# Moving the routing steps of a recurrence-and-experts kernel to fixed places, and moving scatters, gathers and weights ahead of a branch

## The chip, the cores and the metric

The kernel runs on one core of one Trainium2 chip. Five engines work beside each other on that core: TensorE (PE in the profile, with its weight loads listed as PEld), VectorE (DVE), ScalarE (ACT), GpSimd (POOL) and SyncE (SP), which issues most of the DMAs. Each engine runs its own instructions in order and waits on the others by semaphores. The metric is the time of one execution on the device in microseconds (us); less is better. The profile also lists the clock that TensorE was granted, as a share of its full 2.4 GHz: 1.00 is 2.4 GHz and 0.50 is 1.2 GHz.

## The reference

Three stages follow one another. The sizes are B=4 batches, H=8 heads, S=768 steps, head size D=48, so 3072 tokens of 384 numbers; E=8 experts with a hidden size of 1024; a last layer with a hidden size of 2048. All is float32.

```python
for t in range(S):                                   # per batch and head: a decayed sum of outer products
    cur = einsum('bhd,bhe->bhde', u * k[t], v[t])
    y[t] = einsum('bhd,bhde->bhe', r[t], state + cur)
    state = w[t][..., None] * state + einsum('bhd,bhe->bhde', k[t], v[t])
x = y rearranged to 3072 x 384
e = argmax(x @ w_gate); gate = softmax(x @ w_gate)[e]; eom = sigmoid(x @ w_output_gate)
for each expert: out[e == expert] = gate * eom[expert] * (relu(x[e == expert] @ w1[expert]) @ w2[expert])
return relu(out @ w_in) ** 2 @ w_out
```

## The kernel before

**Attention in units.** A unit is one batch and one pair of heads: 16 units, four to a batch. The loop `for t in range(-3, LU + 1)` (L803) is a software pipeline: turn `t` does parts of units `t-1`, `t`, `t+1`, `t+2` and `t+3`, each by a call `at(unit, "part")`. In a unit DVE scans the decays (`suf` L686, then a reciprocal and `ff` L694), makes `kT` (L705) and `rA` (L711) from transposes that PE left in the PSUM tile `pt`, scans the states into `St` (L754), sums the bonus `g` (L720) and writes the rows of the output `xr` (L776, "rows_out"). PE makes transposes (L675), the scores `pa` (L741, in two halves), and the results `py` from the scores (L764) and from the states (L770). POOL makes the causal cut of the scores (the two affine selects on `A`, L744), the products `g` (L715, L716) and `gv` (L724). In every turn but the one that follows a batch's first pair of heads, PE transposes parts of `xr` ("turn_x", L675 too) for the routing. The order of instructions on each engine is that of the code.

**Routing in steps.** When a batch is done, `route_steps` (L161) works out for its 768 tokens which expert each goes to, and its place there. It is a generator. Every `yield` ends a step, and the loop of units calls `route_step()` at a few places per turn. The steps are: the product with both gates (`wcat`, L169) into `lt`; its transposes into `lg`; the maximum `mx` and `z`; then `cand`, `m`, `oh` and the scan `inc` (L190 to L197) on DVE; PE's two matmuls `pk` on `inc` and `oh` (L202, L203), which ACT copies to `kv`, and DVE's `zo`, `zs`, `sg` (L208 to L213); the places `ex`, `bof`, `rk`, `dst`, `dsi` (L217 to L225); the factor `tail` (L227 to L229), which ACT copies into `xr` (L231); and the running counts `cum` and `vals`. With that the rows of the batch go to the table `x_rows` in DRAM by six indirect DMAs on POOL (`scatter_step`, L265).

**First block of experts.** After the loop `blkA` gathers 320 rows of expert 0 (three indirect DMAs on POOL, L409) that belong to the first three batches, scales them, turns them (L440) and runs them through the expert: `up(f)` (nine matmuls into `ph`, then ACT's `hh` and DVE's `hl`) and `down(f)` (nine matmuls into `po`) for f = 0 to 7. Under `up` and `down` the fourth batch is routed. The table `under` says which step follows which of them; `conv(f)` there makes the weights of f (ACT writes `w1h`, `w2h`, DVE `w1l`, `w2l`; called a weight pair below). `finish_steps` (called by `fin`) then makes the table of blocks: `key` to `bvals` (L299 to L307), `bei` to `flag` (L310 to L321) and the list of rows `gi` (L280 to L288). `flag` is read by all engines for a branch on a rare case (L916, L917; not taken with these inputs). Behind the branch come the rest of `blkA`, the second block `blk0` and blocks 1 to 7, whose expert numbers are read from `bei`.

## Time and profile before

| | |
|---|---|
| time, three runs | 904.79, 908.29 (median), 912.22 us |
| profiled execution | 910.06 us, span 908.4 us |
| granted TensorE clock, mean | 0.951 |
| busy: PE, DVE, ACT, POOL | 94%, 62%, 42%, 40% of the span |
| attention, routing of three batches | to about 214 us |
| first block and routing of the fourth batch | about 214 to 257 us |
| blocks of experts, then the last layer | about 257 to 500 us, 500 to 908 us |

The profiled execution is a single one, 1.8 us above the median. A share such as PE's 94% is an average over stages; it includes time in which matmuls run at half the clock. The table of windows and the timelines tell more: where an idle time of an engine stands in brackets in a row, it is the time just before that row, with the instruction that ended it.

### The profile page before, as it was taken

How to read it: one execution, taken by the hardware profiler on the slowest of the kernel's cores; microseconds unless marked ns; L12 is line 12 of the kernel's file. 1: busy time of each engine (PE TensorE's matmuls, PEld its weight loads, DVE VectorE, ACT ScalarE, POOL GpSimd, SP SyncE). 2: the span in 40 equal slices, each digit the busy share in tenths (PEclk: the TensorE clock that was granted, in tenths of full speed). 3: DMA queues.
4: the chain of work that ended last, by engine and by line, in shares of the span. 5: the costliest groups of instructions: out<-in, count | busy, mean ns of one | idle time of the engine just before them, and what ended most of it. 6: DMA issues, size and time to landing. Idle time of an engine off the chain costs nothing.

```text
span 908.4 us, 14382 instructions
## 1 busy us (share of the span) xinstructions
PE 850.1 (94%) x5276; PEld 770.1 (85%) x5276; DVE 561.1 (62%) x1087; ACT 377.4 (42%) x793; POOL 363.3 (40%) x398
## 2 busy tenths in 40 slices
PE   5998989996869999989999999999999999999995
PEld 4888879885758898989998889999898899999985
DVE  5779786874636766876882577777874344343342
ACT  4553545514325455454553443434333333333321
POOL 5773755733234435552554532322322122222111
PEclk9997997967979999999999999999999999999998
DMA  9855586101049667866555432223221230231110
GB/s 191 159 106 106 127 218 148 42 27 49 35 148 210 162 142 242 241 182 188 179 183 105 140 112 86 90 70 97 78 70 39 93 105 20 85 105 34 38 44 35
DMA packets 157331, 102.86 MB, mean 113 GB/s; under 512 B 112316, under 2 KB 140908, under 8 KB 157252
## 3 DMA queue, kind: packets, MB, share of 16 engines
q1 hardware_dynamic: 151396, 86.99, 36.6%
q0 software_dynamic: 4912, 14.65, 4.6%
q8 instruction: 43, 0.70, 0.3%
q10 hardware_dynamic: 944, 0.22, 0.1%
q14 instruction: 36, 0.29, 0.1%
HBM read 79.34 MB, written 22.50 MB: 112 GB/s over the span
## 4 chain that ended last, share of the span: by engine, by line
PE 58%; issue 6%; DVE 3%; POOL 2%; DMA 2%; ACT 1%; POOLq 0%; SPq 0%; DVEq 0%; ACTq 0%
PE ph L359 9%; PE ph L360 9%; PE ph L361 9%; PE po L359 8%; PE po L361 8%; PE po L360 8%; PE px L361 2%; PE px L359 2%; PE px L360 2%; PE px L440 1%; DMA wo_f<-caf 1%; DMA x2r<-x_cols 1%; POOL out_dram L1142 1%; DVE gg L1120 0%; ACT gh L353 0%
## 5 line engine op out<-in xcount | busy, mean ns | idle before, releaser
L1120 DVE SCALAR_TENSOR_TENSOR gg<-ph,rl 128x512 f32<-128x512 f32 x96 | 66.2, 690 | 114.3 <-ACT rl L1118 114.0
L1118 ACT ACTIVATE rl<-ph 128x512 f32<-128x512 f32 x96 | 57.4, 598 | 159.2 <-PE ph L361 156.7
L354 DVE TENSOR_TENSOR gl<-gg,gh 128x512 fp32r<-128x512 f32 x96 | 66.7, 695 | 65.9 <-ACT gh L353 43.3
L353 ACT CAST gh<-gg 128x512 fp32r<-128x512 f32 x96 | 59.6, 621 | 88.9 <-DVE gg L1120 88.9
L354 POOL TENSOR_TENSOR w1l<-w1r,w1h 128x384 fp32r<-128x384 f32 x56 | 59.8, 1075 | 77.6 <-ACT w1h L353 77.5
L350 ACT ACTIVATE hh<-ph 128x320 fp32r<-128x320 f32 (+7 forms) x64 | 32.4, 506 | 117.7 <-PE ph L361 116.4
L359 PE MATMUL po<-hh,w2h 128*128 128x320 f32 (+7 forms) x192 | 69.5, 362 | 6.9 <-DVE yT L483 5.2
L354 DVE TENSOR_TENSOR w2l<-w2r,w2h 128x384 fp32r<-128x384 f32 x64 | 62.5, 978 | 20.8 <-ACT w2h L353 19.1
L351 DVE SCALAR_TENSOR_TENSOR hl<-ph,hh 128x320 fp32r<-128x320 f32 (+7 forms) x64 | 36.8, 575 | 51.2 <-ACT hh L350 51.1
L360 PE MATMUL po<-hl,w2h 128*128 128x320 f32 (+7 forms) x192 | 67.4, 351 | 0.7 <-DVE hl L351 0.5
L361 PE MATMUL po<-hh,w2l 128*128 128x320 f32 (+7 forms) x192 | 67.2, 350 | 0.0
L1066 POOL TENSOR_TENSOR caf<-caf,cbf 128x384 f32<-128x384 f32 x32 | 32.4, 1014 | 52.7 <-DVE cbf L1065 52.6
L764 PE MATMUL py<-vN,A 128*128 128x48 f32 x384 | 52.1, 299 | 0.0
L764 PEld LDWEIGHTS py<-vN,A 128*128 128x128 f32 x384 | 51.4, 218 | 0.1
L1142 POOL DMA_INDIRECT out_dram<-ob,tokc x24 | 23.7, 987 | 67.7 <-DVE ob L1141 63.8
L359 PEld LDWEIGHTS po<-hh,w2h 128*128 128x128 f32 x192 | 36.5, 190 | 10.1 <-DVE yT L483 6.6
L744 POOL TENSOR_SCALAR_AFFINE_SELECT A<-A 128x768 f32<-128x768 f32 x32 | 27.8, 869 | 42.2 <-ACT A L743 38.4
L741 PE MATMUL pa<-rA,kT 64*128 64x128 f32 x384 | 37.4, 326 | 1.3 <-ACT A L743 1.3
L743 ACT COPY A<-pa 128x384 f32<-128x384 f32 x64 | 27.6, 483 | 26.6 <-PE pa L741 26.2
L360 PEld LDWEIGHTS po<-hl,w2h 128*128 128x128 f32 x192 | 36.5, 190 | 2.4 <-DVE hl L351 1.4
L705 DVE TENSOR_TENSOR kT<-pt,suf 128x384 f32<-128x384 f32 x32 | 16.3, 549 | 34.7 <-PE pt L675 34.7
L265 POOL DMA_INDIRECT x_rows<-xr,dsi x24 | 24.5, 1022 | 32.6 <-ACT xr L231 28.9
(802 smaller groups left out, 2556.0 us busy)
## 6 DMA issues: line engine op xcount, KB each, us to landing
w1r<-in_moe_w_dram SPq DMA_DIRECT2D x16, 768.0 KB, 6.6
w2r<-in_moe_w_dram SPq DMA_DIRECT2D x16, 768.0 KB, 8.5
x2r<-x_cols SPq DMA_DIRECT2D x12, 768.0 KB, 5.2
cq<-in_moe_w_in_dram SPq DMA_DIRECT2D x16, 384.0 KB, 5.8
cq<-in_moe_w_out_dram SPq DMA_DIRECT2D x16, 384.0 KB, 5.1
wD<-in_w_dram SPq DMA_DIRECT2D x32, 144.0 KB, 3.5
kN<-in_k_dram SPq DMA_DIRECT2D x32, 144.0 KB, 3.6
rN<-in_r_dram SPq DMA_DIRECT2D x32, 144.0 KB, 3.1
```

The lines of the kernel that those rows point to most:

```text
L350: nc.scalar.activation(hi, src, AF.Relu)
L351: nc.vector.scalar_tensor_tensor(lo, src, 0.0, hi.bitcast(F32), op0=ALU.max, op1=ALU.subtract)
L353: nc.scalar.copy(hi, src)
L354: lo_eng.tensor_tensor(lo, src, hi.bitcast(F32), op=ALU.subtract)
L359: nc.tensor.matmul(out_, a_of(ah), b_of(bh), start=start, stop=False)
L360: nc.tensor.matmul(out_, a_of(ah), b_of(bl), start=False, stop=False)
L361: nc.tensor.matmul(out_, a_of(al), b_of(bh), start=False, stop=stop)
L741: nc.tensor.matmul(pa[j][:, ci], self.kT[pp, hf * HC + ci], self.rA[pp, hf * HC + ci], start=True, stop=True)
L764: nc.tensor.matmul(self.py[j][:, c], self.A[:, c, j], self.vN[:, c, j, :D], start=c == 0, stop=False)
L1118: nc.scalar.activation(rl, ph, AF.Relu)
L1120: nc.vector.scalar_tensor_tensor(gg, ph, 0.0, rl, op0=ALU.max, op1=ALU.mult)
L1142: ins = nc.gpsimd.indirect_dma_start(out=out[:, :], out_offset=IndirectOffsetOnAxis(ap=tokc[:, n:n + 1], axis=0), in_=ob, in_offset=None)
```

## The change

The change touches the places of existing work; no arithmetic of the case at hand is added. Each `yield` of the routing now carries a name ("turn", "scan", "rows", "mid", "end"), and `route_step(name)` in the loop of units runs a step only if the routing waits at that name. The steps `mx`, `z` and `cand` to `inc` become one step. The six scatters of the third batch stand in a row at the end of turn 14. All of `xr`'s transposes of the last unit stand ahead of those of `blkA`. Of the first block seven instead of six `up` stand ahead of the branch, and each of the weight pairs up to f = 7; so do the gather of `blk0` and the load of half of block 1's weights. The instruction that held the loads of the experts until the gather (`bel`, L1178) is gone.

```diff
@@ -50,7 +50,7 @@
     KF2 = F2 // 128
     CAPS = (128, 480, 440, 416, 404, 396, 388, 384)
     NA = 320
-    FA = 6
+    FA = 7
     NTL = 4
     XC = 480
     NXB = 8
...
@@ -169,21 +168,20 @@
                 nc.tensor.matmul(pl[32 * g:32 * g + 32, :GW], wcat[:, c], xT[:, c, g * GW:(g + 1) * GW], start=c == 0, stop=c == KD - 1)
         lt = wk.tile([96, GW], F32, name="lt")
         nc.scalar.copy(lt, pl[:96, :GW])
-        yield
+        yield 'turn'
         lg = wk.tile([128, 2 * E, NTB], F32, name="lg")
         pl = ps_t.tile([128, 512], F32, name=pn)
         for i in range(GW // 128):
             nc.tensor.transpose(pl[:, 96 * i:96 * i + 96], lt[:, 128 * i:128 * i + 128], ident[:96, :96])
         nc.scalar.copy(lg.rearrange("p m (g i) -> p i g m", g=NG),
                        pl[:, :192].rearrange("p (i g m) -> p i g m", i=2, g=NG)[:, :, :, :2 * E])
-        yield
+        yield 'scan'
         gl, ol = lg[:, :E], lg[:, E:]
         bce = lambda t: t.rearrange("p (o t) -> p o t", o=1).to_broadcast([128, E, NTB])
         mx = wk.tile([128, NTB], F32, name="mx")
         nc.vector.tensor_reduce(mx, gl.rearrange("p e t -> p t e"), axis=AX.X, op=ALU.max)
         z = wk.tile([128, E, NTB], F32, name="z")
         nc.vector.tensor_tensor(z, gl, bce(mx), op=ALU.subtract)
-        yield
         ez = wk.tile([128, E, NTB], F32, name="ez")
         nc.scalar.activation(ez, z, AF.Exp)
         cand = wk.tile([128, E, NTB], F32, name="cand")
...
@@ -196,7 +194,7 @@
         inc = wk.tile([128, E, NTB + 1], F32, name="inc")
         nc.vector.tensor_tensor_scan(out=inc.rearrange("p e t -> p (e t)"), data0=rst.rearrange("p e t -> p (e t)"),
                                      data1=ohx.rearrange("p e t -> p (e t)"), initial=0.0, op0=ALU.mult, op1=ALU.add)
-        yield
+        yield 'rows'
         pk = ps_t.tile([128, 512], F32, name=pn)
         pkv = pk[:, :E * (NTB + 1)].rearrange("p (e t) -> p e t", t=NTB + 1)
         nc.tensor.matmul(pkv, ones, inc, start=True, stop=False)
...
@@ -211,7 +209,7 @@
         sg = wk.tile([128, 2, NTB], F32, name="sg")
         nc.vector.tensor_reduce(sg[:, 0], ez.rearrange("p e t -> p t e"), axis=AX.X, op=ALU.add)
         nc.vector.tensor_scalar(sg[:, 0], sg[:, 0], 1e-9, None, op0=ALU.add)
-        yield
+        yield 'scan'
         nc.scalar.activation(sg[:, 1], zs, AF.Exp, scale=-1.0)
         ex = wk.tile([128, E], F32, name="ex")
         nc.vector.tensor_tensor_scan(out=ex, data0=ones[:, :E], data1=kv[:, :, NTB], initial=float(1 + b * S), op0=ALU.mult, op1=ALU.add)
...
@@ -223,15 +221,15 @@
         nc.vector.tensor_reduce(dst, rk.rearrange("p e t -> p t e"), axis=AX.X, op=ALU.add)
         dsi = wk.tile([128, NTB], I32, name="dsi", bufs=2)
         nc.vector.tensor_copy(dsi, dst)
-        yield
+        yield 'rows'
         nc.vector.tensor_scalar(sg[:, 1], sg[:, 1], 1.0, None, op0=ALU.add)
         nc.vector.reciprocal(sg, sg)
         nc.vector.tensor_tensor(tail[:, b, :, 0], sg[:, 0], sg[:, 1], op=ALU.mult)
-        yield LIGHT
+        yield 'mid'
         nc.scalar.copy(xr[:, :, DM:], tail[:, b])
         for c in range(NTB):
             scatters.append((xr, dsi, c, ordered))
-        yield
+        yield 'turn'
         eng = nc.gpsimd if b < B - 2 else nc.vector
         eng.tensor_tensor(cum[:, b + 1], cum[:, b], kv[:, :, NTB], op=ALU.add)
...
@@ -461,12 +459,13 @@
             self.prep_w1(f, eng, hi=hi1)
             self.prep_w2(f, eng2 or eng, hi=hi2)
-        def up(self, f):
+        def up(self, f, into=None):
             half, fo = divmod(f, KF // 2)
             ph = ps_h.tile([128, 512], F32, name="ph")
             for c in range(KD):
                 three(ph[:, :self.cap], self.w1t[half], self.x[c], lambda t: t[:, c, fo * 128:(fo + 1) * 128], lambda t: t, c == 0, c == KD - 1)
-            self.h[f] = split([self.P.hb.tile([128, 512], F32R, name="h" + q)[:, :self.cap] for q in "hl"], ph[:, :self.cap], nc.vector, relu=True)
+            self.h[f] = split(into or [self.P.hb.tile([128, 512], F32R, name="h" + q)[:, :self.cap] for q in "hl"],
+                              ph[:, :self.cap], nc.vector, relu=True)
         def down(self, f, again=False):
             half, fo = divmod(f, KF // 2)
...
@@ -581,10 +582,10 @@
     routing = []
-    def route_step(light=False):
-        if routing and (routing[0][1] or not light):
-            routing[0][1] = next(routing[0][0], 0)
-            if routing[0][1] == 0:
+    def route_step(place=None):
+        if routing and place in (None, routing[0][1]):
+            routing[0][1] = next(routing[0][0], None)
+            if routing[0][1] is None:
                 routing.pop(0)
     with ExitStack() as actx:
...
@@ -820,43 +821,41 @@
                 if t == LU:
                     blkA.prep_w(1, nc.vector)
                 scatter_step(t >= LU - 2)
-                if t == LU - 1:
-                    scatter_step(True)
-                route_step()
+                route_step("turn")
                 at(t, "bonus_v")
                 at(t - 1, "results")
                 at(t, "turn_back_k")
                 at(t + 1, "scan_back")
-                route_step()
+                route_step("scan")
                 at(t, "scores", 0)
                 if t == LU:
                     blkA.scale()
                 at(t - 1, "results_of_states")
                 at(t + 1, "scan_on")
+                route_step("rows")
                 at(t - 1, "rows_out")
                 scatter_step(t >= LU - 2)
                 at(t + 3, "clamp")
                 at(t, "scores", 1)
-                route_step()
-                if t == LU:
-                    blkA.prep_x(0)
-                    blkA.prep_x(1)
+                route_step("mid")
                 at(t + 2, "turn_w")
                 at(t - 1, "turn_x")
+                if t == LU:
+                    for c in range(KD):
+                        blkA.prep_x(c)
                 at(t, "states")
-                if t < LU:
-                    route_step(True)
+                route_step("end")
                 scatter_step(t >= LU - 2)
-                if t == LU - 1:
+                if t == LU - 2:
                     while scatters:
                         scatter_step(True)
+                if t == LU - 1:
                     blkA.gather()
                     blkA.prep_w(0, nc.vector)
                     nc.vector.tensor_reduce(vs, viol, axis=AX.X, op=ALU.add)
                 if t == LU:
                     pf = ps_t.tile([128, 512], F32, name="pt")
                     nc.tensor.matmul(pf[:1, :1], ones[:, 0:1], vs, start=True, stop=True)
-                    blkA.prep_x(2)
                     nc.vector.tensor_scalar(flag[:, 0:1], pf[:1, :1], 0.0, None, op0=ALU.is_le)
                     for f in (2, 3):
                         blkA.prep_w(f, nc.vector)
...
@@ -872,23 +871,31 @@
         last = finish_steps()
         fin = lambda: next(last, None)
         conv = lambda f: blkA.prep_w(f, nc.vector)
+        blocks = [block_of(P, 0, 0)]
+        blk0 = blocks[0]
+
+        def load_next():
+            blocks.append(block_of(P, 1, expert_of(1)))
+            blocks[1].load(0)
+
         under = {
-            ("up", 0): [route_step],
             ("up", 1): [route_step],
-            ("up", 2): [route_step, route_step, lambda: conv(4)],
+            ("down", 0): [route_step],
+            ("up", 2): [route_step],
             ("down", 1): [route_step],
-            ("up", 3): [route_step],
-            ("down", 2): [route_step, route_step],
-            ("up", 4): [route_step, lambda: conv(5)],
-            ("down", 3): [fin],
-            ("up", 5): [fin, lambda: conv(6)],
-            ("down", 4): [fin],
+            ("up", 3): [route_step, route_step],
+            ("down", 2): [route_step, lambda: conv(4)],
+            ("up", 4): [fin],
+            ("down", 3): [lambda: conv(5)],
+            ("up", 5): [fin, load_next],
+            ("down", 4): [lambda: conv(6)],
+            ("up", 6): [fin, blk0.gather, lambda: conv(7)],
         }
         for f in range(FA + 1):
             for what in ("up", "down"):
                 n = f if what == "up" else f - 1
-                if not 0 <= n < FA:
+                if not 0 <= n < (FA if what == "up" else FA - 1):
                     continue
                 getattr(blkA, what)(n)
                 for do in under.get((what, n), ()):
...
@@ -1162,28 +1170,18 @@
                 convert_store(n - 2)
     with tc.manual_schedule(engines={ET.PE, ET.DVE, ET.Activation, ET.SP}):
-        blocks = [block_of(P, 0, 0)]
-        blk0 = blocks[0]
         blk0.w1t, blk0.w2t = blkA.w1t, blkA.w2t
-        blk0.gather()
         atA = [column(offA, i) if i else 0 for i in range(blkA.nt)]
-        blkA.ps_w, blkA.w_name = ps_x, "px"
-        blkA.prep_w(7, nc.vector)
-        for f in range(FA, KF):
-            blkA.up(f)
-            if f > FA:
-                blkA.down(f - 1)
-            if f == KF - 2:
-
-                nc.vector.scalar_tensor_tensor(bel, blk0.xg.bitcast(I32)[0:1, 0, :E], 0, bei, op0=ALU.bitwise_and, op1=ALU.bitwise_or)
-                for k in range(1, E):
-                    blocks.append(block_of(P, k, expert_of(k, True)))
-                blocks[1].load(0)
-                blocks[1].load(1)
-                convert_load(0)
-            if f == KF - 1:
-                blk0.prep_x(0)
+        for blk in (blkA, *blocks):
+            blk.ps_w, blk.w_name = ps_x, "px"
+        blkA.up(KF - 1)
+        blocks[1].load(1, expert_of(1))
+        for k in range(2, E):
+            blocks.append(block_of(P, k, expert_of(k)))
+        convert_load(0)
+        blkA.down(KF - 2)
         blocks[1].gather()
+        blk0.prep_x(0)
         blkA.down(KF - 1)
         blkA.evac()
         for c in range(1, KD):
```


The order of instructions moves at these places.

**DVE, first routed unit of a batch (turns 5, 9 and 13).** `lg`, `cand`, `oh` and `inc` belong to the routing, `suf`, `ff`, `xr`, `kT` to the units. Before:

```order
L183 TENSOR_REDUCE mx<-lg 128x6
L185 TENSOR_TENSOR z<-lg,mx 128x48
L692 RECIPROCAL ff<-suf_147 128x6
L694 SCALAR_TENSOR_TENSOR ff<-wz_145,ff,psU 128x127 x6
L776 TENSOR_TENSOR xr<-py,gv 128x6x48 x2
L190 SCALAR_TENSOR_TENSOR cand<-z,e_514 128x48
L192 TENSOR_REDUCE m_1132<-cand 128x6
L195 TENSOR_TENSOR oh_72<-cand,m_1132 128x8x6
L197 SCALAR_TENSOR_TENSOR inc<-rst,oh_72 128x56
L705 TENSOR_TENSOR kT<-pt,suf_147 128x384 x2
```

With the change:

```order
L182 TENSOR_REDUCE mx<-lg 128x6
L184 TENSOR_TENSOR z<-lg,mx 128x48
L188 SCALAR_TENSOR_TENSOR cand<-z,e_513 128x48
L190 TENSOR_REDUCE m_1087<-cand 128x6
L193 TENSOR_TENSOR oh_72<-cand,m_1087 128x8x6
L195 SCALAR_TENSOR_TENSOR inc<-rst,oh_72 128x56
L693 RECIPROCAL ff<-suf_146 128x6
L695 SCALAR_TENSOR_TENSOR ff<-wz_144,ff,psU 128x127 x6
L206 TENSOR_TENSOR zo<-lg,oh_72 128x48
L208 TENSOR_REDUCE zs<-zo 128x6
L210 TENSOR_REDUCE sg<-ez 128x6
L211 TENSOR_SCALAR sg<-sg 128x6
```

The four instructions `cand` to `inc` moved from behind `xr` to ahead of the reciprocal and `ff`, and `zo` to `sg`, which stood ahead of the next unit's `suf`, now follow `ff`; `xr` and `kT` come after them. On PE the two matmuls on `inc` and `oh` moved with them, from behind the transposes of `rN` to between the two halves of the scores.

**DVE, second routed unit (turns 6, 10 and 14).** `dsi` ends the places of the rows; `tail` is the factor of each row. Before:

```order
L225 CAST dsi<-dst 128x6
L692 RECIPROCAL ff<-suf_148 128x6
L694 SCALAR_TENSOR_TENSOR ff<-wz_146,ff,psU 128x127 x6
L776 TENSOR_TENSOR xr<-py,gv 128x6x48 x2
L227 TENSOR_SCALAR sg<-sg 128x6
L228 RECIPROCAL sg<-sg 128x12
L229 TENSOR_TENSOR tail<-sg 128x6
L705 TENSOR_TENSOR kT<-pt,suf_148 128x384 x2
```

With the change:

```order
L223 CAST dsi<-dst 128x6
L693 RECIPROCAL ff<-suf_147 128x6
L695 SCALAR_TENSOR_TENSOR ff<-wz_145,ff,psU 128x127 x6
L225 TENSOR_SCALAR sg<-sg 128x6
L226 RECIPROCAL sg<-sg 128x12
L227 TENSOR_TENSOR tail<-sg 128x6
L777 TENSOR_TENSOR xr<-py,gv 128x6x48 x2
L706 TENSOR_TENSOR kT<-pt,suf_147 128x384 x2
```

The three instructions that make `tail` moved ahead of `xr`, for which PE's transposes of "turn_x" wait.

**POOL, turns 14 and 15.** The `L265`/`L262` rows are the scatters of the third batch, `gv` and the affine selects belong to the last unit. Before:

```order
L265 DMA x_rows<-xr,dsi 3073x386
L724 TENSOR_TENSOR gv<-vN_144,g 128x576
L744 AFFINE_SELECT A<-A 128x768
L263 MEMSET oh_72 1x1
L265 DMA x_rows<-xr,dsi 3073x386
L744 AFFINE_SELECT A<-A 128x768
L263 MEMSET oh_72 1x1
L265 DMA x_rows<-xr,dsi 3073x386
```

With the change:

```order
L262 DMA x_rows<-xr,dsi 3073x386
L260 MEMSET oh_72 1x1
L262 DMA x_rows<-xr,dsi 3073x386
L725 TENSOR_TENSOR gv<-vN_143,g 128x576
L260 MEMSET oh_72 1x1
L745 AFFINE_SELECT A<-A 128x768 x2
L407 DMA xg<-x_rows,gA 128x386 x2
L407 DMA xg<-x_rows,gA 64x386
```

All scatters of the batch now stand ahead of the last `gv`, and between it and the gathers of the first block (the two last rows) are one small memset and the two affine selects. Before, scatters stand on both sides of the affine selects, and one more (not shown) between these rows and the gathers.

## Rows read from the trace of the kernel before

**Rows 1.** Windows: us, busy PE, PEld, DVE, ACT, POOL, granted clock, DMA share, GB/s.

```profile
80.00:85.00 5.00, 4.91 (x27) 4.75 (x27) 4.93 (x14) 0.20 (x1) 1.15 (x1) 0.62 0.90 175
85.00:90.00 5.00, 5.00 (x36) 4.67 (x37) 4.36 (x16) 1.91 (x5) 0.00 (x0) 0.50 0.02 3
90.00:95.00 5.00, 5.00 (x35) 4.61 (x34) 1.29 (x5) 2.18 (x6) 2.40 (x3) 0.51 0.00 0
200.00:205.00 5.00, 5.00 (x45) 4.83 (x45) 4.85 (x13) 0.59 (x2) 3.17 (x4) 0.93 0.31 119
```

**Rows 2.** Timeline of PE: the first matmul of `py<-vN,A` (L764) in three units running.

```profile
81.04 5.14 PE L764 MATMUL py<-vN,A 128*128 128x48 f32 x24
...
97.36 2.78 PE L764 MATMUL py<-vN,A 128*128 128x48 f32 x24
...
107.97 2.22 PE L764 MATMUL py<-vN,A 128*128 128x48 f32 x19
```

**Rows 3.** Timeline of PE: five first matmuls after an idle stretch, which stands in brackets.

```profile
63.80 0.88 PE L675 MATMUL pt<-ident,xr 128*128 128x128 f32 x6 [0.45 <-DVE xr L776]
...
80.09 0.55 PE L675 MATMUL pt<-ident,rN 128*128 128x128 f32 x3 [2.52 <-DVE kT L705]
...
208.42 0.88 PE L675 MATMUL pt<-ident,xr 128*128 128x128 f32 x6 [0.97 <-DVE xr L776]
...
347.83 0.45 PE L359 MATMUL po<-hh,w2h 128*128 128x416 f32 x1 [1.48 <-DVE yT L483]
...
486.12 0.44 PE L359 MATMUL po<-hh,w2h 128*128 128x384 f32 x1 [1.67 <-ACT hh L350]
```

**Rows 4.** Two source lines of the routing: shortest, median and longest of four instructions, in ns.

```profile
L197 DVE TENSOR_TENSOR_SCAN inc<-rst,oh x4: 274/1504/1511, 78.1 to 237.9; 128x56 f32<-128x56 f32 x4
...
L213 DVE TENSOR_SCALAR sg<-sg x4: 172/691/693, 83.3 to 239.7; 128x6 f32<-128x6 f32 x4
```

**Rows 5.** Timeline of DVE: routed units of the first batch; last row, the fourth batch.

```profile
75.95 0.72 DVE L190 SCALAR_TENSOR_TENSOR cand<-z,e 128x48 f32<-128x48 f32 x1
...
85.79 0.14 DVE L217 TENSOR_TENSOR_SCAN ex<-ones,kv 128x8 f32<-128x8 f32 x1
...
87.02 0.19 DVE L692 RECIPROCAL ff<-suf 128x6 f32<-128x6 f32 x1
...
91.91 0.16 DVE L227 TENSOR_SCALAR sg<-sg 128x6 f32<-128x6 f32 x1
...
92.37 0.17 DVE L229 TENSOR_TENSOR tail<-sg 128x6 f32<-128x6 f32 x1
...
237.12 0.21 DVE L190 SCALAR_TENSOR_TENSOR cand<-z,e 128x48 f32<-128x48 f32 x1
```

**Rows 6.** Timelines of POOL and PE around the last two units and the first up().

```profile
208.64 0.89 POOL L744 TENSOR_SCALAR_AFFINE_SELECT A<-A 128x768 f32<-128x768 f32 x1
...
217.31 0.92 POOL L409 DMA_INDIRECT xg<-x_rows,gA  x1 [0.30 <-issue]
...
220.69 2.29 PE L440 MATMUL pt<-ident,xg 128*128 128x128 f32 x6 [6.60 <-ACT xg L430]
...
223.47 0.62 PE L359 MATMUL ph<-x0h,w1h 128*128 128x320 f32 x1
...
232.80 0.39 PE L359 MATMUL po<-hh,w2h 128*128 128x320 f32 x1
```

**Rows 7.** Timelines of DVE and PE ahead of the branch and behind it.

```profile
243.70 0.49 DVE L351 SCALAR_TENSOR_TENSOR hl<-ph,hh 128x320 fp32r<-128x320 f32 x1 [0.60 <-ACT hh L350]
...
248.18 0.48 DVE L351 SCALAR_TENSOR_TENSOR hl<-ph,hh 128x320 fp32r<-128x320 f32 x1
...
250.64 0.54 DVE L354 TENSOR_TENSOR w1l<-w1r,w1h 128x384 fp32r<-128x384 f32 x1
...
251.57 0.17 DVE L280 TENSOR_TENSOR tva<-slot,bvals 128x32 f32<-128x32 f32 x1
...
257.21 0.61 PE L359 MATMUL ph<-x0h,w1h 128*128 128x320 f32 x1 [7.06 <-DVEq L917]
```

More of the change, by code (lines that the diff above doesn't have):

```diff
@@ L97, in rwkv_moe_kernel @@
     bei = cst.tile([1, E], I32, name="bei")
-    bel = cst.tile([1, E], I32, name="bel")
     tail = cst.tile([128, B, NTB, 2], F32, name="tail")
@@ L255, in route_steps @@
             nc.vector.tensor_copy(vals[:, 0], cum[:, B])
-    LIGHT = 1
     scatters = []
@@ L398, in rows, with load @@
             return min(128, self.cap - 128 * i)
-        def load(self, hf):
-            self.w1r[hf], self.w2r[hf] = load_expert(self.P.raw, self.w1e, self.w2e, hf)
+        def load(self, hf, e=None):
+            if e is not None:
+                self.w1e, self.w2e = w1[ds(e, 1)], w2[ds(e, 1)]
+            self.w1r[hf], self.w2r[hf] = load_expert(self.P.raw, self.w1e, self.w2e, hf, (self.w1r[hf], self.w2r[hf]) if hf in self.w1r else None)
         def gather(self, xg=None, tiles=None):
@@ L538, in again @@
             for f in range(upto):
-                self.up(f)
-                self.down(f, True)
+                self.up(f, self.h[upto - 1 - (upto - 1 - f) % 3])
+                if f < upto - 1:
+                    self.down(f, True)
         def whole(self, at):
@@ L566, in column, with expert_of @@
         return nc.values_load(t[0:1, k:k + 1], engines=(ET.SP,), min_val=0, max_val=NCOL - 128 if t is offA else NT)
-    def expert_of(k, late=False):
-        return nc.values_load((bel if late else bei)[0:1, k:k + 1], engines=(ET.SP,), min_val=0, max_val=E - 1)
+    def expert_of(k):
+        return nc.values_load(bei[0:1, k:k + 1], engines=(ET.SP,), min_val=0, max_val=E - 1)
     mctx = ExitStack()
@@ L785, in turn_x @@
                 if self.pr == HP - 1:
-                    routing.append([route_steps(self.b, xTs[self.b], xrs[self.b], rw, ps_t), LIGHT])
+                    routing.append([route_steps(self.b, xTs[self.b], xrs[self.b], rw, ps_t), 'end'])
         blkA = first_block(P)
@@ L978, in rwkv_moe_kernel @@
             put_ids_A()
-            blkA.ps_w, blkA.w_name = ps_x, "px"
+            blk0.gather(blk0.xg)
+            blocks[1].load(0, expert_of(1))
         nx = nc.values_load(flag[0:1, 1:2], min_val=0, max_val=NXB)
```

6 lines of the change are left out of this document (2 added, 4 removed).

## The prediction

> **What bounds the kernel now.** I read the clock and the busy shares by window first, then the starts of like matmuls on the timeline of PE, then each idle time of PE with what ended it, and last the source lines of the routing. PE bounds nearly all of it; what the change can move is the time in which PE idles or runs at half clock before about 270 us. Around the first batch's routing PE is busy throughout 80 to 95 us, but at 0.62, 0.50 and 0.51 of its clock [rows 1]: against full clock that is 5 x (0.38 + 0.50 + 0.49) = 6.9 us of work lost. The reader is to see in the starts of `py` that a unit takes 107.97 - 97.36 = 10.61 us undisturbed, and 97.36 - 81.04 = 16.32 us when it holds the low stretch [rows 2]. Ahead of that stretch PE idled 2.52 us for `kT` [rows 3]; two more like it (2.53 and 2.51 us) follow in the second and third batches, each with such a stretch behind it, the third's until 200.7, since 0.93 of 200 to 205 is 0.7 us at half [rows 1]. The other places are the junction between the last unit and the first block (6.60 us idle, for the gathered rows [rows 6]) and the branch (7.06 us [rows 7]).
>
> What made `kT` late is DVE: `cand` begins at 75.95 [rows 5] and the scan `inc` ends at 78.1 + 1.51 = 79.6 [rows 4], 3.65 us for four small instructions. In the fourth batch, with POOL idle, `cand` begins at 237.12 [rows 5] and `inc` ends at 237.9 + 0.27 = 238.2 [rows 4]: 1.05 us. The Trainium skill (SBUF — State Buffer, Who interferes with whom) says that a DVE instruction with two SBUF inputs contends with a GpSimd instruction that reads SBUF, and that the one issued first holds the other up. The trace agrees, 1.51 against 0.27 us; by the rule the order of two instructions within a few tenths of a us decides the next part's tie.
>
> **First routed unit, three times.** `cand` to `inc` now follow `z`, in a stretch of some 2 us in which POOL waits for the scores. They cost 1.05 us there instead of 3.65, and `zo` to `sg`, four instructions of about 0.2 (the last 0.17 when nothing stretches it [rows 4]), come in as 0.8: `py` of the next unit would start at 81.04 - 3.65 + 1.05 + 0.8 = 79.2. PE's two matmuls on `inc` go between the halves of the scores and delay the second affine select by about 0.6, to just the moment at which `zo` starts. If the select is first, `zo` waits for most of its 0.89 [rows 6] and the last of the four is stretched by 0.5 [rows 4]: 80.4 then, some 1.2 later. The two are a tie, so I take the middle: **-1.2 us**, ends -0.6 and -1.8. PE's idle time here falls from 2.5 to between 0.5 and 1.7.
>
> **Second routed unit, three times.** PE waits in a plain unit 0.45 us for `xr` [rows 3]. Ahead of `xr` stand `ex` to `dsi` as before (87.02 - 85.79 = 1.23), and now the three instructions of `tail` too (92.37 + 0.17 - 91.91, about 0.6) [rows 5]. So PE idles here 0.45 + 1.23 + 0.55 = 2.2 us, and up to 3.1 if the first of the three is stretched as L213 was, or waits for a select. In before, this wait of 1.7 was hidden since PE ran at half clock and was late itself. The unit takes 10.61 + 1.23 + 0.55 = 12.4 us at full clock, against 16.32: **-3.9**. POOL's next instruction is the scatter, which waits for ACT's copy of `tail`, so it stretches no more of this.
>
> Whether the clock stays is the main question. Gaps of 0.97 and 1.48 us were followed by no fall; gaps of 1.67 and 2.52 were [rows 3]. 2.2 lies among those that mostly were. A fall gives back up to the 6.9 us above; 6.2 is my estimate, since part of such a stretch lies beside work that DVE bounds. A batch that keeps its clock is then worth -1.2 - 3.9 = **-5.1 us**, one that falls after the new gap 6.2 - 5.1 = **+1.1 us**. The Trainium skill (TensorE: Matmul & The Clock Gate, What's actually happening) says that how many matmuls run at the lower clock at a kernel's start differs from run to run of one kernel. By it the same gap can cost a low stretch in one execution and not in the next, so that 2.5 us need not have fallen each time either; the profile is of one execution, but the three times of before agree, 7.4 us apart.
>
> **Junction.** The gathers were issued up to 217.31 and the first `ph` ran at 223.47 [rows 6]. With the scatters done in turn 14, POOL reaches the gathers after the second select, 208.64 + 0.89 = 209.5, so the last is issued at about 212 and lands at 214.6 by the 2.6 us that the last one took before. PE ends the results of the last unit at 220.69 - 6.60 = 214.1, waits about 1 for `xr`, then turns `xr` and `xg`; the first `ph` comes at 217.5 to 218.4. The product `wcat`, now inside the first `up`, is followed by the same `up(1)`; the first `po` comes at 223.0 (full clock) to 225.0 (half), against 232.80: -9.8 to -7.8, I take the middle, **-8.8**.
>
> From the first `po` to PE's resumption behind the branch were 257.21 - 232.80 = 24.4 us [rows 7]. Now DVE's chains each have a weight pair behind them, and the `up` that needs it, with its `hl`, follows that; DVE waits about 1.2 for each. The `hl` at 243.70 (10.9 behind the first `po`) should come at 10.2. To the next, the 4.48 between 243.70 and 248.18 loses 0.7 of counts and gains 1.2: 5.0. Then `hl` and the chain `bei` to `flag`, 250.64 - 248.18 = 2.46, half a pair, 0.5, and the rest of the `up` and its `hl`, 1.7: 4.6. Then `hl`, 0.4, the list of rows, the load of the flag and the branch, 257.21 - 251.57 = 5.64, and one more pair, 251.57 - 250.64 = 0.93: 7.0 [rows 7]. In all 26.8, so +2.4; without the two waits 0, with a third 3.7. I take **+3.0**. For that, one `up` less stands behind the branch: 1.33 us at full clock, 2.4 at half, **-1.9**. Block 1's weights come earlier, which hides behind PE except for a gap of 0.3: **-0.2**. POOL and SP, which now gather and load ahead of the branch, have to be done before it; both bounds are near (0 to +1, as the gather of 0.9 runs beside the last pair): **+0.5**. Removing `bel` and the order of the rare path cost nothing on the path: DVE's 0.14 us lies in a wait. The junction sums to -8.8 + 3.0 - 1.9 - 0.2 + 0.5 = **-7.4**, ends about -11 and -3.5. Everything behind 300 us is the same, within 1 us.
>
> **The sum.** Against the profiled execution of 910.1 us (1.8 above the median of 908.3): all three batches fall, 910.1 - 7.4 + 3 x 1.1 = 906.0; one keeps its clock, 899.8; two, 893.6; three, 887.4. The three runs of before lie 912.2 - 904.8 = 7.4 us apart, about what one such stretch costs, which speaks for falls that come in some executions only; so I expect a mixture, and one that keeps it as likelier than two.
>
> **The rivals.** (1) *All three still fall*, since the gap at the second routed unit takes the place of the one removed: 906. For it: the gap of 2.2 lies above 1.67; against it: it is shorter than the 2.5 of before. (2) *All three keep the clock*: 887. For it: the gap is shorter than any before it in the units; against it 1.67 [rows 3]. (3) *The chains ahead of the branch eat the junction's gain*: three waits, a half-clocked first block and POOL late give -2 in place of -7.4, so 905 with one batch kept and 911 with all fallen. For it: DVE has every pair and chain in one row; against it, the gathers' 5 us of lead. (4) *Slower*: the instruction that starts `tail` is caught by a select or a product of POOL, the gap becomes about 3 us, and the low stretch lasts as long as the third batch's, from 183.4 behind its gap to 200.7, 17 us in place of some 14, in every batch: 1.1 + 0.9 + 1.7 = +3.7 a batch, 910.1 - 7.4 + 11.1 = 913.8 (it decides once the three batches give back more than the junction's 7.4). If besides the junction only gives -3.5, 917.7.
>
> **How the numbers follow.** Forecast, one or two keep the clock: 0.40 (of it one, 899.8, 0.24). Rival 1: 0.30. Rival 2: 0.12. Rival 3: 0.08. Rival 4: 0.10. The predicted time is 900. The range 887 to 911 leaves out half of rival 2, all of rival 4 and a little of rival 3. One per cent of 908.3 is 9.1 us, about what a measurement tells here: faster is below 899.2, slower above 917.4. Faster: 0.12 + 0.16 and over half of the 0.24, 0.42; slower: 0.06; within: 0.52.
>
> **What would show it.** In the profile after: `cand` to `inc` in about 1 us right behind `z`; PE's idle time for `kT` under 1.7 in the first routed units and about 2.2 for `xr` in the second; granted clock 1.0 in the windows behind at least one of them; the gathers of the first block issued near 210 to 212 and the first `po` at 223 to 225 of the old scale less what the batches gained; a wait of 6 to 7 us at the branch still. Wrong would be the forecast if the clock falls behind gaps of a microsecond too, or if DVE's chains are late already under the first `up`.

## The result and the profile after

The changed kernel took 898.41 us (median of nine runs, 889.24 to 901.11) against 907.96 us (nine runs, 904.49 to 912.22): a ratio of 0.9872, 95% interval 0.9832 to 0.9913. The forecast was 900, range 887 to 911. The total came where it was expected; its parts did not, and the sections below are about that.

The profiled execution is one of 898.41 us, mean granted clock 0.968 against 0.951. Its span, from the page:

```profile
span 896.7 us, 14396 instructions
```

**Batches.** The windows of the changed kernel, with the columns of [rows 1]:

```profile
85.00:90.00 5.00, 3.20 (x33) 2.56 (x31) 2.26 (x8) 3.43 (x8) 3.75 (x5) 0.75 0.10 40
...
90.00:95.00 5.00, 5.00 (x42) 4.83 (x42) 4.70 (x11) 1.12 (x5) 3.74 (x5) 0.90 1.01 212
...
135.00:140.00 5.00, 5.00 (x45) 4.91 (x42) 3.31 (x6) 2.42 (x5) 4.42 (x8) 0.66 0.88 197
...
200.00:205.00 5.00, 4.02 (x28) 3.77 (x29) 0.82 (x2) 1.57 (x4) 0.00 (x0) 0.50 0.03 0
```

A low stretch is time at a granted clock of 0.50. The clock still falls in each second routed unit (0.75 and 0.90; 0.66), but for 3.4 us in the first two batches and 6.8 in the third, where it stayed down for 13.6 us of 80 to 95 before [rows 1]. In the last window it is down altogether: a stretch of 17.1 us lies over the junction. The starts of `py` on the timeline of PE, as [rows 2]:

```profile
78.17 2.78 PE L765 MATMUL py<-vN,A 128*128 128x48 f32 x24
...
91.44 2.78 PE L765 MATMUL py<-vN,A 128*128 128x48 f32 x24
...
102.00 2.78 PE L765 MATMUL py<-vN,A 128*128 128x48 f32 x24
...
124.72 2.78 PE L765 MATMUL py<-vN,A 128*128 128x48 f32 x24
...
138.12 3.08 PE L765 MATMUL py<-vN,A 128*128 128x48 f32 x24
```

The two last rows hold the second routed unit of the second batch. In the first batch the two routed units took 10.39 us (67.78 to 78.17) and 13.27 us; before, 12.40 and 16.32. From the start of the first routed unit to the end of the second the three batches took 28.72, 28.72 and 29.22 us before and 23.66, 23.79 and 24.85 now: -5.06, -4.93 and -4.37. PE's idle times in the units, as [rows 3]:

```profile
77.78 0.55 PE L676 MATMUL pt<-ident,rN 128*128 128x128 f32 x3 [0.30 <-DVE kT L706]
...
87.02 1.08 PE L676 MATMUL pt<-ident,xr 128*128 128x128 f32 x6 [1.80 <-DVE xr L777]
...
133.93 0.88 PE L676 MATMUL pt<-ident,xr 128*128 128x128 f32 x6 [2.15 <-DVE xr L777]
...
180.21 1.54 PE L676 MATMUL pt<-ident,xr 128*128 128x128 f32 x6 [2.59 <-DVE xr L777]
...
194.89 0.88 PE L676 MATMUL pt<-ident,xr 128*128 128x128 f32 x6 [2.48 <-DVE xr L777]
```

The wait for `kT` is 0.30 us in place of 2.52; the waits for `xr` in the second routed units are 1.80, 2.15 and 2.59. The last row is new: in turn 15 PE idled 2.48 us for `xr`, 0.97 before [rows 3]. The two source lines that answer to [rows 4], now L195 and L211:

```profile
L195 DVE TENSOR_TENSOR_SCAN inc<-rst,oh x4: 274/274/275, 72.8 to 218.1; 128x56 f32<-128x56 f32 x4
...
L211 DVE TENSOR_SCALAR sg<-sg x4: 173/477/481, 76.1 to 220.2; 128x6 f32<-128x6 f32 x4
```

`inc` takes 0.274 us in all four batches (up to 1.51 before), and `L211` is stretched to 0.48 where L213 was to 0.69.

**Junction and branch.** POOL and PE, as [rows 6]:

```profile
193.23 0.87 POOL L745 TENSOR_SCALAR_AFFINE_SELECT A<-A 128x768 f32<-128x768 f32 x1 [0.86 <-ACT A L744]
...
196.84 1.28 POOL L407 DMA_INDIRECT xg<-x_rows,gA  x1 [0.31 <-issue]
...
204.75 1.54 PE L676 MATMUL pt<-ident,xr 128*128 128x128 f32 x6 [0.98 <-DVE xr L777]
...
208.77 0.63 PE L355 MATMUL ph<-x0h,w1h 128*128 128x320 f32 x1
...
215.78 0.39 PE L355 MATMUL po<-hh,w2h 128*128 128x320 f32 x1
```

The gathers are issued 0.43 us behind the last start of `py` (196.41 to 196.84 for the third), so the rows no longer hold PE: it waits 0.98 us for `xr`, not 6.60 for them. But from 196.77 to 213.84 this ran at half clock. Behind the branch, timelines of PE, POOL and DVE:

```profile
243.35 0.60 PE L355 MATMUL ph<-x0h,w1h 128*128 128x320 f32 x1 [5.66 <-DVEq L924]
...
249.05 0.93 POOL L407 DMA_INDIRECT xg<-x_rows,gi  x1 [0.30 <-issue]
...
255.04 0.17 DVE L418 COPY xid<-xg 128x3 f32<-128x3 f32 x1 [4.14 <-DMA xg<-x_rows,gi]
...
255.71 2.88 DVE L426 TENSOR_SCALAR xg<-xg 128x384 f32<-128x384 f32 x4
...
256.18 0.33 PE L438 MATMUL px<-ident,xg 128*128 128x128 f32 x1 [1.57 <-DVE xg L426]
```

The wait at the branch is 5.66 us (7.06 before [rows 7]). Then something new: the last gather of block 1, issued at 249.05, let DVE go on only at 255.6, DVE's scaling of those rows took 2.88 us for four tiles, and PE idled 1.57 us for it, and twice 0.74 more.

The difference of the two profiled spans, 896.7 - 908.4 = -11.7, in pieces: -0.9 ahead of the first routed unit; -14.4 in the three batches; -0.1 in the units between; +1.8 in turn 15 (8.75 to 10.59 us); -3.5 from there to the first `po` (22.86 to 19.37); +3.2 to PE's first matmul behind the branch, called its resumption (24.41 to 27.57); +2.2 from there to the end (651.2 to 653.4). This is one execution; a second one, below, divides otherwise behind the batches.

### The profile page after: what moved, and what is told of

Same layout as the page of the kernel before. It is cut to its first block, busy times and chain, and to the rows that moved or that the text cites. A ratio compares the mean times of both kernels' runs of the same rounds, so it can differ in the third digit from the quotient of the medians.

```text
span 896.7 us, 14396 instructions
## 1 busy us (share of the span) xinstructions
PE 840.2 (94%) x5276; PEld 760.2 (85%) x5276; DVE 555.9 (62%) x1086; ACT 377.7 (42%) x793; POOL 363.9 (41%) x398
## 4 chain that ended last, share of the span: by engine, by line
PE 58%; issue 6%; DVE 3%; DMA 2%; POOL 2%; ACT 1%; POOLq 0%; SPq 0%; DVEq 0%; ACTq 0%
PE ph L356 9%; PE ph L357 9%; PE ph L355 9%; PE po L355 8%; PE po L357 8%; PE po L356 8%; PE px L357 2%; PE px L355 2%; PE px L356 2%; DMA wo_f<-caf 1%; PE px L438 1%; DMA xg<-x_rows,gi 1%; DMA x2r<-x_cols 1%; POOL out_dram L1150 0%; DVE caf L1070 0%
## 5 line engine op out<-in xcount | busy, mean ns | idle before, releaser
L350 DVE TENSOR_TENSOR w2l<-w2r,w2h 128x384 fp32r<-128x384 f32 x64 | 63.0, 985 | 19.5 <-ACT w2h L349 18.4
L765 PE MATMUL py<-vN,A 128*128 128x48 f32 x384 | 47.4, 283 | 0.0
L355 PEld LDWEIGHTS po<-hh,w2h 128*128 128x128 f32 x192 | 37.4, 195 | 11.7 <-DVE yT L482 6.6
L765 PEld LDWEIGHTS py<-vN,A 128*128 128x128 f32 x384 | 47.1, 202 | 0.1
L407 POOL DMA_INDIRECT xg<-x_rows,gi x28 | 28.2, 1008 | 32.0 <-PE px L438 12.8
L357 PEld LDWEIGHTS po<-hh,w2l 128*128 128x128 f32 x192 | 37.5, 195 | 1.1
L695 DVE TENSOR_TENSOR_SCAN ff<-wz,ff,psU 128x127 f32<-128x127 f32 x96 | 37.2, 457 | 0.6
L262 POOL DMA_INDIRECT x_rows<-xr,dsi x24 | 23.9, 996 | 32.6 <-ACT xr L229 27.8
```

The costliest lines, as they stand in the source:

```text
L350: lo_eng.tensor_tensor(lo, src, hi.bitcast(F32), op=ALU.subtract)
L355: nc.tensor.matmul(out_, a_of(ah), b_of(bh), start=start, stop=False)
L357: nc.tensor.matmul(out_, a_of(al), b_of(bh), start=False, stop=stop)
L695: nc.vector.tensor_tensor_scan(out=self.fv[:, c, 1:], data0=self.z[:, c, :C - 1], data1=zeros[:, :C - 1], initial=self.fv[:, c, 0:1], op0= ...
L765: nc.tensor.matmul(self.py[j][:, c], self.A[:, c, j], self.vN[:, c, j, :D], start=c == 0, stop=False)
```

## The experiments

Theory A, formed on these rows: all of the gain is in the batches, since the low stretch behind a gap for `xr` is short; the rest of the change nets about nothing. Theory B is the sum on record. Each ratio is to the kernel before on the same chip, with its 95% interval; the kernel before ran at medians of 904.3 to 905.2 us there.

**One half of the change at a time.** The routing's new places alone, in the kernel before (the other calls and the named yields likewise):

```diff
-                route_step()
+                route_step("turn")
```

> The kernel before with the routing steps alone at their new places in the units; scatters, gathers, the table under the first block and everything behind it stay as before. Theory A (all of the gain is in the three routed batches: 24 us from one py to the next but one instead of 28.7, about -4.7 us each): about 894 to 896 us against 908, ratio 0.985 to 0.988, as fast as the whole change. Theory B (the batches give little and the junction 7.4 us, as the prediction's sum has it for one batch that keeps its clock): about 905, ratio 0.996. By both the profile has the gap of 2.5 us for kT gone and one of about 2.2 us for xr in the second routed unit.

And all but that (the old calls, all of them, in the changed kernel):

```diff
-                route_step("turn")
+                route_step()
```

> The changed kernel with the routing steps of the units back at their old places; scatters in a row, gathers, table, weights and loads ahead of the branch stay as changed. Theory A (the rest of the change nets about zero: some 3.5 us won up to the first po, 3.2 lost up to the branch, 2.2 lost behind it): 906 to 911 us, ratio 0.998 to 1.003. Theory B (junction -7.4): about 901, ratio 0.992.

The batches alone gave 895.83 us, 0.9907 (0.9871 to 0.9944); the rest alone 910.93 us, 1.0066 (1.0040 to 1.0093), slower. Theory A is the nearer one, though both ratios came out above its ranges; Theory B's 0.996 and 0.992 lie outside the intervals. But the halves don't add up: -8.5 and +6.6 us make -1.8, and the whole gives about -10. In the second kernel `tail` is late as before, and the six scatters that now stand in a row wait for it; its turn 15 took 12.84 us, against 8.75 before and 10.59 in the change (first two rows below). What stretches it so far is not shown. So this kernel prices the rest of the change beside the old places only. Beside the new ones it is the whole against the batches alone: 0.9872 and 0.9893 against 0.9907, nothing clear of the noise. In the second kernel the gap for `kT` is back too, and the low clock behind it (timeline of PE, then a window):

```profile
198.36 2.78 PE L768 MATMUL py<-vN,A 128*128 128x48 f32 x24
...
211.20 5.36 PE L768 MATMUL py<-vN,A 128*128 128x48 f32 x24
...
130.10 0.55 PE L679 MATMUL pt<-ident,rN 128*128 128x128 f32 x3 [2.53 <-DVE kT L709]
...
135.00:140.00 5.00, 5.00 (x37) 4.67 (x36) 4.36 (x16) 1.78 (x5) 0.00 (x0) 0.50 0.88 224
```

**The change again, and one step of it.** The change unedited first:

> The changed kernel itself, unedited, beside the next three on the same chip. Both theories: 889 to 901 us as before; its profile shows whether the low stretches behind the gaps for xr (3.4, 3.4 and 6.8 us at half clock) and the one over the junction (17 us) come in every execution. Theory A (low stretches behind gaps differ from run to run): another mix of lengths. Rival (they are fixed by the program): the same four lengths.

It gave 894.50 us, 0.9893 (0.9823 to 0.9962); the profiled execution, 888.69 us, is the fastest of its four. The gaps for `xr` were the same to 0.01 us (1.80, 2.15, 2.60), what followed was not: 3.4 us, none and 3.4 us at half clock, and 10.2 over the junction. Its second batch:

```profile
126.58 2.78 PE L765 MATMUL py<-vN,A 128*128 128x48 f32 x24
...
135.79 0.88 PE L676 MATMUL pt<-ident,xr 128*128 128x128 f32 x6 [2.15 <-DVE xr L777]
...
138.90 2.78 PE L765 MATMUL py<-vN,A 128*128 128x48 f32 x24
...
135.00:140.00 5.00, 4.21 (x49) 3.75 (x49) 2.94 (x8) 3.89 (x9) 4.22 (x4) 1.00 0.73 167
```

So the same gap in the same program is followed by a fall in one execution and not in the next, and the second profile prices the fall: this unit took 138.90 - 126.58 = 12.32 us without one, and 138.12 - 124.72 = 13.40 with one in the first profile, 1.1 us more.

Behind the batches the two executions differ more. Here turn 15 lost 0.6 us in place of 1.8 (its gap was 1.05 us, not 2.48), the first `po` came 6.7 us sooner behind the last `py` than before, in place of 3.5, PE's resumption cost 2.8 in place of 3.2, and from there to the end it was 2.6 us less than before (648.5) in place of 2.2 more. The batches gave 16.3 us. The gap of 2.48 us in turn 15 came behind a low stretch of 6.8 us in turn 14, that of 1.05 behind 3.4; this is not shown to be the cause, as `tail_end_held` below has 2.48 behind 3.4.

`cand` to `inc` alone (with ACT's `ez`, which stands among them), moved up in the kernel before:

```diff
         nc.vector.tensor_tensor(z, gl, bce(mx), op=ALU.subtract)
-        yield
...
                                      data1=ohx.rearrange("p e t -> p (e t)"), initial=0.0, op0=ALU.mult, op1=ALU.add)
         yield
+        yield
```

> The kernel before with cand to inc alone moved up behind z (three times); the two matmuls on them, zo to sg, tail, and all else stay where they were. Theory A (the stretched four instructions ahead of kT are what PE's 2.5 us and the long low stretches come from): the gap for kT falls under 0.6 us and 9 to 13 us go, ratio 0.985 to 0.99, nearly the whole of the change. Rival (each of the moved steps counts, and zo to sg ahead of the next suf makes xr as late as tail does): a gap for xr of about 2 us in the second routed unit, with low stretches of 13 us behind it again: 4 us or less gained, ratio above 0.995.

892.83 us, 0.9866 (0.9812 to 0.9920): four instructions, moved three times, give as much as the whole change. On PE:

```profile
76.92 0.79 PE L750 MATMUL psU<-vN,kP 128*64 128x48 f32 x20 [0.70 <-DVE ff L694]
...
79.78 2.84 PE L764 MATMUL py<-vN,A 128*128 128x48 f32 x24
...
88.99 1.54 PE L675 MATMUL pt<-ident,xr 128*128 128x128 f32 x6 [2.08 <-DVE xr L776]
```

The gap for `kT` went, as Theory A has it. There is a small one of 0.70, and the rival's gap for `xr` came too: 2.08 us in two batches and 2.88 in the third. The rival's loss did not come: what followed was 6.8 us, none and 3.4 us at half clock, in place of 13.

**The load behind the branch.** The load of block 1's second half held until its last gather has landed:

```diff
-        blocks[1].load(1, expert_of(1))
...
+        nc.vector.scalar_tensor_tensor(bel, blocks[1].xg.bitcast(I32)[0:1, blocks[1].nt - 1, :E], 0, bei, op0=ALU.bitwise_and, op1=ALU.bitwise_or)
         blocks[1].scale(nc.vector)
+        blocks[1].load(1, nc.values_load(bel[0:1, 1:2], engines=(ET.SP,), min_val=0, max_val=E - 1))
```

> The changed kernel, with the load of the second half of block 1's weights held until the last of that block's gathers has landed (as the removed instruction bel held the loads of before). Theory A (that load, issued between the gathers, is what makes the last gather land 5.9 us behind its issue instead of 3.1, and DVE's scaling and PE wait for it: gaps of 1.57 and twice 0.74 us): the landing is back at about 3 us, the gaps go, 2 to 3 us less than the changed kernel, about 895.5. Rival (the scaling on DVE is late by itself, or the gathers are late because they only start behind the branch): the gaps stay, the same time as the changed kernel.

> The kernel of load_held once more, beside the next three. Theory A (holding the load takes DVE's wait for the last gather away, 2 to 3 us, whatever the clock does): the scaling of block 1's rows starts with no wait for the DMA in the profile, 2 to 3 us below the changed kernel, ratio to the kernel before about 0.985. Rival (887 of load_held came from an execution without a long low stretch over the junction): ratio 0.989, the same as the changed kernel's.

887.65 us, 0.9874 (0.9784 to 0.9963; three runs at 887, one at 900), and 887.38 us, 0.9798 (0.9761 to 0.9836). POOL's last gather and DVE, first in the unedited change (its second profile), then in the second run with the load held:

```profile
244.77 0.94 POOL L407 DMA_INDIRECT xg<-x_rows,gi  x1 [0.30 <-issue]
...
249.98 0.15 DVE L418 COPY xid<-xg 96x1 f32<-96x1 f32 x1 [0.31 <-DMA xg<-x_rows,gi]
```

```profile
244.30 0.93 POOL L407 DMA_INDIRECT xg<-x_rows,gi  x1 [0.30 <-issue]
...
248.45 0.15 DVE L1189 SCALAR_TENSOR_TENSOR bel<-xg,bei 1x8 int32<-1x8 int32 x1 [2.24 <-DMA xg<-x_rows,gi]
248.56 0.22 DVE L418 COPY xid<-xg 128x3 f32<-128x3 f32 x2
...
248.70 1.41 DVE L426 TENSOR_SCALAR xg<-xg 128x384 f32<-128x384 f32 x4
```

DVE went on from the rows 4.26 us behind the issue of the last gather; in the two profiles of the change it was 6.57 and 5.21. The wait for the gather is shorter, not gone: the added instruction `bel` waits 2.24 us for it, where DVE had waited 4.14 and 0.41 in the first profile of the change and 3.29 and 0.31 in the second. PE's idle times for the scaled rows (1.57 and twice 0.74 us in the first profile, 0.62 in the second) are gone. The scaling took 1.41 us, but it took 1.40 in the second profile of the change as well, with the load not held: the 2.88 of the first came with a `w1l` on POOL beside two of its four tiles. From PE's resumption to the end were 646.6 us, against 653.4 and 648.5 in the two profiles of the change. Theory A holds for the mechanism: with the load held DVE has the last gather's rows sooner. The medians differ by 7 us; the profiles show 1.9 to 6.8 us in this place, and the intervals of the two ratios overlap, so the size stays between 2 and 7.

**The places in turn 15 and of `tail`.** The counts of the third batch behind `xr`:

```diff
-        yield 'turn'
+        yield 'turn' if b != B - 2 else 'late'
...
                 at(t - 1, "rows_out")
+                route_step("late")
```

> The changed kernel with the counts and the list of rows of the third batch (turn 15) on DVE behind the unit's xr instead of ahead of it; all else as changed. Theory A (PE's idle 2.48 us for xr in that turn is what the half-clock stretch of 17 us over the junction follows): the gap falls under 1 us, granted clock 1.0 from 195 to 210, the first po 3 to 6 us sooner, time 3 to 6 us less than the changed kernel, 892 to 895. Rival (the gap comes of PE's low clock in the second routed unit of that batch, or the low stretch comes from the wait for the gathered rows): the gap or the low stretch stays, and the gathers, issued later by about 0.8 us, make it the same or 1 us slower.

895.69 us, 0.9916 (0.9884 to 0.9949), no gain. The gap for `xr` went, but PE then waited 0.57 us for `St` and 1.17 for the gathered rows, and 10.2 us ran at half clock all the same. The rival is the better account. Then `tail` behind `xr` (`tail_late`, shown here), and `ex` to `dsi` with it (`places_late`, where the step named 'late' begins ahead of `ex`):

```diff
         nc.vector.tensor_copy(dsi, dst)
-        yield 'rows'
+        yield 'late'
```

> The changed kernel with tail's three instructions behind xr again, as before the change. Theory A (the gap for xr is 0.45 + 1.23 + 0.55 us and its size sets whether the clock falls): gaps of about 1.3 to 1.7 in place of 1.8, 2.15 and 2.6; 0.55 us for each batch, and about 1 us more for each low stretch that no longer comes: 2 to 5 us less than the changed kernel. Rival (tail catches POOL's products there and makes kT late): a gap for kT appears in that unit, no gain or a loss of 2 us.

> The changed kernel with ex to dsi and tail of the first three batches behind xr, in the 2 to 3.6 us that DVE idles there ahead of kT. Theory A: the gap for xr in the second routed unit falls to a plain unit's 0.45, no low stretch follows it, kT has no gap above 0.6; a batch takes about 21.2 us from py to the next but one instead of 23.7 to 24.9, so 7 to 9 us less than the changed kernel, 886 to 890 where that is at 895. Rival (the nine instructions are stretched by POOL's products and make kT late): a gap for kT of 1.5 to 3 us with low stretches of 13 us behind it, as in the kernel before: 5 to 15 us slower than the changed kernel.

`tail_late` gave 893.03 us, 0.9865 (0.9810 to 0.9920), the same as the change: PE's wait in the first two batches became two, 1.18 us for `xr` and 0.97 for ACT's copies of `wz`. `places_late` gave 898.10 us, 0.9925 (0.9886 to 0.9964). Neither theory had the reason, which the timelines of ACT and PE show:

```profile
88.58 0.20 ACT L232 COPY xr<-tail 128x12 f32<-128x12 f32 x1 [2.70 <-DVE tail L230]
...
88.68 0.85 ACT L685 COPY wz<-pt 128x384 f32<-128x384 f32 x2
...
89.21 0.90 PE L679 MATMUL pt<-ident,xr 128*128 128x128 f32 x3 [2.65 <-ACT wz L685]
```

The change had moved ACT's copy of `tail` ahead of its copies of `wz`. With `tail` later, ACT waited 2.70 us for it, `wz` stayed in PSUM, and PE's transposes of `xr` waited 2.65 us for that tile. So the copy went to the end of the turn, where the kernel before had it, with the load held:

```diff
-        yield 'mid'
+        yield 'end' if b < B - 1 else 'mid'
```

> As places_late, with ACT's copy of tail into xr at the end of the turn, behind its copies of wz and xT, as it stood before the change; the load held as in load_held. Theory A (in places_late ACT waited 2.7 us for tail ahead of its copies of wz, and PE's transposes of xr waited for those): no gap above 0.6 us in the second routed unit, about 21.2 us from one py to the next but one, no low stretch there; 7 to 10 us below the changed kernel, ratio about 0.977. Rival (kT is late then, by DVE's nine instructions): a gap for kT of 1 to 2.5 us in place of that for xr, and a ratio of 0.985 or more.

> As places_end_held, with the counts and the list of rows of the third batch behind xr of turn 15 too. Theory A (the gap for xr in that turn is 1.05 us where no low stretch comes before it, and goes; but the gathers are issued about 0.8 us later and PE waits for the rows then): within 2 us of places_end_held. Rival (that gap is what the low stretch over the junction follows): 3 us or more below it.

> As tail_late, with ACT's copy of tail at the end of the turn and the load held. Theory A: the wait for wz (0.97 us) goes, PE waits once, about 1.2 to 1.7 us, for xr; 3 to 5 us below the changed kernel, ratio about 0.983, between load_held and places_end_held. Rival (gaps of 1.2 us and 2.2 us are followed by low stretches alike): the ratio of load_held.

`places_end_held` gave 883.72 us, 0.9754 (0.9717 to 0.9791); with the counts late too it was 885.72 us, 0.9769 (0.9732 to 0.9807); with only `tail` behind `xr` 888.65 us, 0.9811 (0.9773 to 0.9850). Theory A of the first holds: PE in the first batch, and at the last unit:

```profile
80.38 2.78 PE L768 MATMUL py<-vN,A 128*128 128x48 f32 x24
...
90.57 0.55 PE L679 MATMUL pt<-ident,rN 128*128 128x128 f32 x3 [0.33 <-DVE kT L709]
...
90.96 2.78 PE L768 MATMUL py<-vN,A 128*128 128x48 f32 x24
...
101.56 2.67 PE L768 MATMUL py<-vN,A 128*128 128x48 f32 x23
...
187.84 4.90 PE L768 MATMUL py<-vN,A 128*128 128x48 f32 x24 [1.10 <-POOL A L748]
```

From `py` to the next but one it is 101.56 - 80.38 = 21.2 us, 10.6 each, with no gap above 0.44; the third batch has one of 0.88, and none of the three a low stretch. This kernel beats the change by about 1.2% of the time (0.9754 against 0.9872 and 0.9893, intervals that don't meet). The held load has its share in that: against the load held alone (0.9798) the moved steps give 0.4%, 3.7 us, with intervals that overlap. The counts late gave nothing more, as Theory A of that run has it. With only `tail` behind `xr` the time is the rival's, that of the load held alone (0.9811 and 0.9798), though not for its reason: the gaps of 1.2 us in two batches had no fall behind them, and what was won there may have gone again in turn 15, where a gap of 2.48 us and then 17.1 us at half clock came. In the last unit of `places_end_held` PE waited 1.10 us for POOL's select, and 17.1 us at half clock followed over the junction, as in the change.

## Why the prediction was right in sum and wrong in its parts

**First routed unit: the mechanism right, the size too small.** 79.2 or 80.4 was given for the next `py`; the row 78.17 is 10.39 us behind the unit's start at 67.78, which is 79.0 on the scale of before. Of the tie, `zo` came first (75.42, the select at 75.65); `inc` is at 0.274, and the gap at 0.30. But the sum took the middle of the two, -1.2 us, and the three batches gave -2.0, -2.3 and -2.4 here, beyond the nearer end of -1.8.

**Second routed unit: the gap right, its price mis-sized.** The gaps of 1.80, 2.15 and 2.59 answer to 0.45 + 1.23 + 0.55 = 2.2, and the unit of 12.32 us of the second profile of the change, where no fall came, to 12.4. The step that failed is the term "A fall gives back up to the 6.9 us above; 6.2 is my estimate". It was taken from stretches behind a gap for `kT`. Behind a gap for `xr` of 2.15 us the fall cost 13.40 - 12.32 = 1.1 us (3.4 us at half clock), and the 6.8 us of the third batch cost 14.46 - 12.4 = about 2. So a batch that fell was worth -4.4 to -5.3 us and the one that kept its clock -6.0, where +1.1 and -5.1 were forecast. In the first profile all three fell: by the prediction's cases that is 906, and it took 898.4. That falls come in some executions only was right. The trace of before already held a short fall, behind a gap smaller than the 1.48 us that the prediction names as followed by none (PE, then a window; a mean clock of 0.66 over 5 us is 3.4 us at half):

```profile
509.67 0.45 PE L359 MATMUL po<-wo3h,gh 128*128 128x384 f32 x1 [1.43 <-ACT gh L353]
...
510.00:515.00 5.00, 4.89 (x18) 4.18 (x17) 3.65 (x5) 2.92 (x7) 4.26 (x5) 0.66 0.00 0
```

**Junction: the gathers right, the clock given too little.** The lead of the gathers came as forecast. The term -8.8 for the first `po` measured -3.5 in the first profile and -6.7 in the second. It had 13 to 15 us from the last `py` to the first `po` (223.0 at full clock, 225.0 at half); measured were 19.4 us with 17.1 at half clock in the change, and 16.2 to 16.5 in four profiles with 10.2 at half clock (18.4 in `counts_late`, which had as much and two waits more). One of the prediction's own signs of being wrong is here: in the second profile of the change this stretch came with no gap above 1.05 us ahead of it in turns 15 and 16. And before it, turn 15 lost 1.8 us (0.6 in the second profile), which no term held: PE waited for `xr`, which DVE makes behind the counts. In `counts_late`, where `xr` comes first, that gap is gone.

**Ahead of the branch: right.** +3.0 was given, and +3.2 and +2.8 measured. The steps are right as well: 10.2, 5.0, 4.6 and 7.0 were given, and DVE's `hl` and PE's resumption came at 10.8, 5.5, 4.8 and 6.4. PE idled 0.98, 2.39 and 0.63 us for weight pairs, and 5.66 at the branch.

**Behind it: a cost set to nothing.** "Removing `bel` and the order of the rare path cost nothing on the path" failed, as far as `bel` goes. With `bel` the load of the weights had waited for a gather; without it both ran at once, and the rows came late: 5.1 to 6.6 us from the last gather's issue until DVE went on in the six profiles without the hold, 3.7 to 4.3 in the five with it. -1.9 - 0.2 was the forecast; +2.2 was measured in the first profile and -2.6 in the second. From the resumption to the end the five profiles with the load held have 646.6 to 650.8 us, the six of the new order without it 648.5 to 654.2, the three of the old order 648.0 to 651.8; the `up` that is gone may be worth what was said, but these ranges overlap.

**The total.** It was right by luck. In the first profile, which lies at the median, 11.5 us too little in the batches (14.4 measured, 2.9 forecast) met 11.1 too much from turn 15 on (-7.4 forecast, 1.8 - 3.5 + 3.2 + 2.2 = +3.7 measured). Of the 11.5 the first routed units make 3.1 and the price of the falls nearly all the rest. In the second profile the batches gave 16.3 us and everything from turn 15 on -5.9, near the forecast; nothing made up for the batches, and the time was 888.7. How many batches keep their clock, the forecast's question, moved the time by about 1 us each.

## What to carry to other kernels

A few tiny instructions between two that matter can cost an engine more than long ones elsewhere: look for the same line with a minimum far from its median, and move it to where the engine that slows it is idle. In this kernel the price of an idle time of PE depended more on where it lay than on its size: take the length of the low stretch from a gap at the same place, and from more than one execution. When an instruction is moved behind a wait, follow what stands behind it on its own engine, and ask of each hold that is removed what it had kept apart.

## What had not been expected of the hardware

Gaps of PE of 2.5 us ahead of the transposes of `rN` and `py` were followed by 6.8 to 17.1 us at half clock in six cases of six; gaps of 1.80 to 2.88 us ahead of the transposes of `xr` in a second routed unit by none, 3.4 or 6.8 us in twenty-five cases, the same gap differently from one execution to the next (2.15 us: three falls in six). What in the work behind the gap makes the difference was not tried. Over the junction 6.8 to 20.5 us ran at half clock in each profile, also behind gaps of only 1.0 to 1.1 us; what starts that is open too. With two loads of weights issued beside four gathers of rows, DVE went on 5.1 to 6.6 us behind the last gather's issue (249.05 to 255.62 at most), and 4.3 us at most with the loads held. DVE's scaling of the rows took 2.88 us beside a `w1l` of 2.22 us on POOL, and 1.41 without one.
